# The last block of each attention unit as 64 by 64 corners, and the natural k of two units turned on chip

## The chip, the core and the metric

The kernel runs on one core of a Trainium2 chip. The core has five engines with queues of their own: TensorE (PE; its weight loads are listed apart, as PEld), VectorE (DVE), ScalarE (ACT), GpSimd (POOL) and SyncE (SP, which issues most transfers). The metric is device time in microseconds for one launch, over several executions; lower is better.

## What is computed

A linear attention with decay over 8 batches, 8 heads, 576 positions and 64 dimensions, whose output is the input of a mixture of eight experts with a fixed capacity of 576 tokens each:

```python
scores = scale * np.matmul(q, k.transpose(0, 1, 3, 2))
Dmat = np.where(rel >= 0, gamma[:, None, None] ** rel[None, :, :], 0.0)   # rel = query position - key position
x = np.matmul(scores * Dmat, v)                      # then (batch, position) rows of 512
# tokens are given to experts in order of their gate logits, 576 to each expert
h = np.maximum(x[mask] @ w1[e], 0.0); out[mask] = h @ w2[e]
```

All of it is in float32.

## The kernel before

The attention is cut into 16 **units** (u): a pair of batches times a pair of heads. A unit's sequence is 9 blocks of 128 columns for each head. Blocks 0 to 7 are 128 positions of one batch, b = 0 and 1 in turn. The last one, block 8, holds the last 64 positions of both batches side by side. q and k come in transposed (`qin`, `kin`: the dimensions of two heads on 128 partitions), v comes in natural form (`vin`), and k a second time in natural form (`nin`, 512 KB a unit), since the running state needs it.

A unit has two **halves**, g = 0 and 1. In half g of unit u TensorE runs, in program order:

- `from_states(u, g)`: what earlier blocks contribute through the running state, q times `st` into the PSUM tile `px` (L713). In half 1 there are 12 matmuls: 8 with 128 columns and 4 with 64 columns, the last four for block 8. Each takes 64 rows and 64 columns of the array, at four places in turn.
- `scores` of the next half (L678: 8 matmuls, 64 rows by 128 columns of the array, two at a time), and in half 0 also of block 8 (L683: 2 matmuls over all 128 by 128 pairs of block 8, into spare columns of `px`).
- `update(n, .)`: two adds of four matmuls to the running state in PSUM (L699); ACT then copies the scaled state to `st` (L702).
- `from_blocks(u, g)`: the masked scores times v into `px` (L722), and in half 1 block 8 too (L728: 4 matmuls over 128 rows and 64 columns).

DVE multiplies the scores by the decay mask (`masks`: L690 into `am` for four blocks, L688 into `at` for block 8, 256 columns). Half of what L683 computes pairs positions of different batches; the mask holds zeros there. ACT copies the finished `px` to `xT` (`keep`, L737). In some halves the gate's logits follow (`logits`, L754) and DVE prepares the routing (`fills`).

POOL scales q (`qscale`, L654) and the natural k (`kscale`, L659, into `ks`) of unit u+2 at the end of unit u. For units 0 and 1 no natural k is loaded: `kscale_pe` turns four blocks of `kin` by TensorE into the PSUM tile `pT` (L667), and DVE scales them into `ks` (L668).

Nothing but the text of the program sets the order: each engine runs its own instructions as they were written, SP's transfers among them, and semaphores hold one engine to another. A tile has a few buffers, and whoever writes a buffer anew waits for the last reader of the old content: `kin`, `qin` and `vin` have 4, `nin` has 3, `px` has 2, `sc` has 1. The loads of unit u+4 are written in unit u: k after the scores of half 0, q and natural k in half 1. v of unit u+3 comes at the start of unit u.

After the 16 units come the routing and the eight experts, each with two layers of matmuls (L1190, L1258).

Of the kernel before, what the change touches and what calls it, by code (L numbers as in the profile page):

```python
# [10 lines left out]
F32 = mybir.dt.float32  # L11
# [3 lines left out]
ALU = mybir.AluOpType  # L15
# [3 lines left out]
B, H, S, D = 8, 8, 576, 64  # L19
NP, HP, NB = 4, 4, 9  # L20
# [4 lines left out]
def consts_np():  # L25
    h = np.arange(H); g = (1.0 - 2.0 ** (-5.0 - h)).astype(np.float64)
    p = np.arange(128); gh = g.reshape(HP, 2)[:, p // 64].T
    i = np.arange(128)
    ex = 0.125 * gh[:, :, None] ** i
    ss = gh[:, :, None] ** (128.0 * np.arange(1, 5))  # L30
    c = np.arange(4)
    ks = g.reshape(HP, 1, 1, 2)[None] ** (-(128.0 * c[None, None, :, None, None] + p[:, None, None, None, None]))
    ks = np.broadcast_to(ks, (128, HP, 4, 2, 2))
    f = lambda a: np.ascontiguousarray(a, dtype=np.float32).reshape(128, -1)
    g1 = g[None] ** (-p[:, None].astype(np.float64)); g2 = g[None] ** (-(p[:, None] % 64).astype(np.float64))
    return np.concatenate([f(a) for a in (ks, ss, g1, g2, ex)], axis=1)

RUNS = ((0, 256, 0), (256, 512, 1), (512, 832, 0), (832, 1152, 1))
# [554 lines left out]
def attention(tc, nc, P, qk, vk, cst_d, wg_d, rf, xd, Lg, raw):  # L593
# [5 lines left out]
    m1, m2 = [cst[:, x:x+1024].rearrange("p (h j q) -> p h j q", h=4, j=2) for x in (NC, NC + 1024)]  # L599
    tri = raw()[:, :128].bitcast(BF16).rearrange("p (m q) -> p m q", m=2)  # L600
    for m in range(2):
        nc.vector.tensor_scalar(tri[:, m], P['it'], 0.0, None, op0=ALU.is_ge)
    nc.vector.memset(tri[:64, 1, 64:], 0.0)

    def decays(hp):
        for m, x in enumerate((80, 88)):
# [64 lines left out]
    def scores(u, g):  # L671

        t = SC[u, g] = P['pp'].tile([128, 2, 512], F32, name="sc", tag="sc")
        k, q = LD[u, 'k'], LD[u, 'q']
        for j in range(4):
            for h in range(2):
                r = slice(64*h, 64*h+64)
                nc.tensor.matmul(t[:, h, 128*j:128*j+128], blk(k, 4*g+j)[r], blk(q, 4*g+j)[r], start=(j == 0), stop=True, skip_group_check=True)  # L678
        if g:
            PX[u, 1] = P['pp'].tile([128, 2, 512], F32, name="px", tag="px", bufs=2)  # L680
            for h in range(2):
                r = slice(64*h, 64*h+64)
                nc.tensor.matmul(PX[u, 1][:, h, 384:], blk(k, 8)[r], blk(q, 8)[r], start=True, stop=True, skip_group_check=True)  # L683

    def masks(u, g):
        if g:
            AT[u] = P['w'].tile([128, 2, 128], F32, name="at", bufs=1)
            nc.vector.tensor_tensor(AT[u], PX[u, 1][:, :, 384:], m2[:, u % HP], op=ALU.mult)  # L688
        a = AM[u, g] = P['w'].tile([128, 2, 4, 128], F32, name="am", bufs=2)
        nc.vector.tensor_tensor(a, SC[u, g].rearrange("p h (j q) -> p h j q", q=128),  # L690
                                m1[:, u % HP, :, None, :].to_broadcast([128, 2, 4, 128]), op=ALU.mult)
# [11 lines left out]

    def from_states(u, g):

        if g == 0:
            PX[u, 0] = P['pp'].tile([128, 2, 512], F32, name="px", tag="px", bufs=2)
        q = LD[u, 'q']
        for c, o, n in ((1, 128, 128),) if g == 0 else ((2, 0, 128), (3, 128, 128), (4, 256, 64)):
            for b, h in ((0, 0), (1, 1), (1, 0), (0, 1)):  # L710
                r, y = slice(64*h, 64*h+64), 64*(h ^ b)
                x = 256*c + 128*b if c < 4 else 1024 + 64*b
                nc.tensor.matmul(PX[u, g][y:y+64, b, o:o+n], SS[u, c-1][r, b], q[r, x:x+n],  # L713
                                 start=(c == 1 + g), stop=False, skip_group_check=True)

    def from_blocks(u, g):
        v = LD[u, 'v']
        for j in range(4):
            c, b = divmod(j, 2)
            for h in range(2):  # L720
                y = 64*(h ^ b)
                nc.tensor.matmul(PX[u, g][y:y+64, b, 128*c:128*c+128], blk(v, 4*g+j)[:, 64*h:64*h+64], AM[u, g][:, h, j],  # L722
                                 start=False, stop=True, skip_group_check=True)
        if g:
            for b in range(2):
                for h in range(2):
                    y = 64*(h ^ b)
                    nc.tensor.matmul(PX[u, g][y:y+64, b, 256:320], blk(v, 8)[:, 64*h:64*h+64], AT[u][:, h, 64*b:64*b+64],  # L728
                                     start=False, stop=True, skip_group_check=True)

    def keep(u, g):
        bp, hp = divmod(u, HP)
# [133 lines left out]
    def ahead(u):  # L866
        if u == 0:
            load(2, "qknv")
            load(3, "qkn")
        if u + 3 < 16:  # L870
            load(u + 3, "v")
        if u == 1:
            R.fetch(nc, rf)
            for b in range(2):
                for h in range(2):
                    nc.sync.dma_start(wg[64*h:64*h+64, :, b, 0:8], wg_d.rearrange("(hp h p) e -> h p hp e", h=2, p=64)[h ^ b])
# [13 lines left out]
    qscale(1, (0, 512))  # L890
    qscale(1, (512, 1024), (1024, 1152))
    last = 15
    for u in range(16):
        ahead(u)
        for g in range(2):
            n, m = (u, u + 1)[g], (1, 0)[g]
            from_states(u, g)
            if u == g == 0:
                update(0, 1)
                kscale_pe(0, 1)  # L900
            if g and u + 4 < 16:
                load(u + 4, "qn")
            if u == 0 and g:
                kscale_pe(1, 1)
            if n <= last:
                scores(n, m)
                masks(n, m)
                update(n, 2 - 2*g)
            elif g:
                here[0] = P['pp'].tile([128, 2, 512], F32, name="px", tag="px", bufs=2)  # L910
                logits(NP-1, 0, 4)
            from_blocks(u, g)
            if u == g == 0:
                kscale_pe(1, 0)
            if not g and u + 4 < 16:
                load(u + 4, "k")
            if n <= last:
                update(n, 3 - 2*g)
            end = u == last and g
            here[0] = PX[u, g]  # L920
            if end:
                keep(u, g)
                R.kp = False
                logits2(NP-1, 0, 4)
                rest(R.count_first(27, 31))
                logits(NP-1, 4, 9, range(HP - 1))
                fills(u, g)
                break
            fills(u, g - 0.5)
            keep(u, g)  # L930
            fills(u, g)
            for f in later:
                f()
            later.clear()
            if g and u + 2 <= last:
                qscale(u + 2, (0, 512), (512, 1024), (1024, 1152))
                kscale(u + 2, 0, 8)
                kscale(u + 2, 8, 16)
    bp = NP-1
    left = [(y, b) for y, x in ((bp - 1, range(6, NB)), (bp, range(NB))) for b in x]  # L940

# [459 lines left out]
```

## Time and profile before

| | us |
|---|---|
| three runs, median (lowest to highest) | 598.72 (597.72 to 598.8) |
| the profiled execution, its own time | 598.47 |
| its span, first to last instruction | 596.3 |
| TensorE busy | 587.7 (99%) |
| VectorE busy | 410.5 (69%) |
| ScalarE busy | 256.4 (43%) |
| GpSimd busy | 242.9 (41%) |
| chain that ended last: share of TensorE | 93% |

The granted TensorE clock is full (9 tenths or more) in all 40 slices of the page. The page's DMA row reads 8 or 9 tenths in the first four slices, and 79.30 MB are read from HBM in all. A busy share tells little by itself here: which engine is waited for is read from the waits and from the chain of work.

### The profile page before, as it was taken

The numbers are of one execution on the slowest core, as the hardware profiler recorded it, in microseconds if no ns is written. First come the engines' busy times: TensorE is split into PE (matmuls) and PEld (weight loads), VectorE is DVE, ScalarE is ACT, GpSimd is POOL, SyncE is SP. The second block draws the span as 40 slices with busy tenths as digits, with TensorE's granted clock in tenths as the row PEclk, the third lists the DMA queues.
The fourth block names the chain that finished last, engine by engine and source line by source line (L and its number), as shares of the span: only waits on it lengthen the run. The fifth ranks groups of instructions, "written<-read, shape, count | busy, mean of one in ns | idle before, by whom it ended". The sixth has DMA issues, their size and how long they took to land.

```text
span 596.3 us, 15107 instructions
## 1 busy us (share of the span) xinstructions
PE 587.7 (99%) x5877; PEld 514.6 (86%) x5877; DVE 410.5 (69%) x1484; ACT 256.4 (43%) x464; POOL 242.9 (41%) x318
## 2 busy tenths in 40 slices
PE   8999999999999999999999999999999999999997
PEld 5888888885798899879988998898789889989976
DVE  5447687896999788878976876788588557543400
ACT  3534333334572664435561654266245334433310
POOL 3777666415311641451342153134214754841012
PEclk9999999999999999999999999999999999999999
DMA  8999999646865897795894699289928833430001
GB/s 329 411 377 406 309 402 370 206 129 229 270 157 111 263 272 158 254 243 146 217 295 143 155 243 255 83 195 245 253 79 192 261 110 102 154 135 27 1 27 53
DMA packets 48745, 123.27 MB, mean 207 GB/s; under 512 B 6946, under 2 KB 19746, under 8 KB 48674
## 3 DMA queue, kind: packets, MB, share of 16 engines
q1 hardware_dynamic: 35554, 79.05, 37.6%
q0 software_dynamic: 12976, 43.00, 31.2%
q8 instruction: 46, 0.75, 0.5%
q10 hardware_dynamic: 144, 0.26, 0.1%
q14 instruction: 25, 0.20, 0.1%
HBM read 79.30 MB, written 18.87 MB: 165 GB/s over the span
## 4 chain that ended last, share of the span: by engine, by line
PE 93%; issue 3%; DMA 2%; POOL 1%; DVE 1%; ACT 0%; POOLq 0%; SPq 0%; DVEq 0%; ACTq 0%
PE ph L1190 35%; PE py L1258 31%; PE sc L678 6%; PE px L722 5%; PE pS L699 3%; PE px L713 3%; PE r L403 2%; PE pt L1145 2%; PE pT L754 2%; PE pT L794 1%; POOL out_y L1215 1%; DMA xg<-xd,idx 1%; PE px L728 1%; DMA raw<-in_w 1%; PE px L683 1%
## 5 line engine op out<-in xcount | busy, mean ns | idle before, releaser
L1258 PE MATMUL py<-w2h,hb 128*128 128x512 f32 x560 | 180.8, 395 | 0.0
L1190 PE MATMUL ph<-xh,w1h 128*128 128x320 f32 (+1 forms) x512 | 152.2, 301 | 0.0
L1190 PE MATMUL ph<-xl,w1h 128*128 128x320 f32 (+1 forms) x512 | 149.2, 296 | 0.0
L1190 PE MATMUL ph<-xh,w1l 128*128 128x320 f32 (+1 forms) x512 | 149.1, 296 | 0.0
L1258 PE MATMUL py<-w2l,hb 128*128 128x512 f32 (+1 forms) x312 | 121.8, 390 | 0.0
L1258 PEld LDWEIGHTS py<-w2h,hb 128*128 128x128 f32 x560 | 102.8, 188 | 21.9
L1194 ACT ACTIVATE hb<-ph 128x256 fp32r<-128x256 f32 (+1 forms) x128 | 52.3, 408 | 106.7 <-PE ph L1190 104.3
L1190 PEld LDWEIGHTS ph<-xh,w1h 128*128 128x128 f32 x512 | 96.2, 190 | 1.1 <-ACT xh L1154 0.5
L1190 PEld LDWEIGHTS ph<-xl,w1h 128*128 128x128 f32 x512 | 96.2, 190 | 0.3
L1190 PEld LDWEIGHTS ph<-xh,w1l 128*128 128x128 f32 x512 | 96.1, 190 | 0.0
L1215 POOL DMA_INDIRECT out_y<-yt,idx x39 | 39.5, 1014 | 117.7 <-ACT yt L1275 58.0
L1199 DVE SCALAR_TENSOR_TENSOR hb<-ph,hb 128x256 fp32r<-128x256 f32 (+1 forms) x192 | 57.9, 350 | 23.8 <-ACT hb L1194 23.3
L1258 PEld LDWEIGHTS py<-w2l,hb 128*128 128x128 f32 (+1 forms) x312 | 55.2, 177 | 12.4
L1275 ACT ACTIVATE yt<-py 128x512 f32<-128x512 f32 x31 | 18.5, 598 | 93.5 <-PE py L1258 61.6
L654 POOL TENSOR_TENSOR qin<-qin,cst 128x512 f32<-128x512 f32 (+2 forms) x47 | 45.3, 991 | 32.2 <-DMA qin<-in_qk 32.2
L702 ACT ACTIVATE st<-pS,cst 128x128 f32<-128x128 f32 x64 | 23.5, 367 | 73.1 <-PE pS L699 73.1
L690 DVE TENSOR_TENSOR am<-sc,cst 128x1024 f32<-128x1024 f32 x32 | 39.0, 1219 | 21.4 <-PE sc L678 17.6
L1070 POOL DMA_DIRECT2D w2l<-raw x24 | 21.6, 902 | 71.7 <-ACT w2l L1069 39.0
L1091 POOL DMA_INDIRECT xg<-xd,quarter x36 | 37.2, 1033 | 18.4 <-ACT hb L1194 7.6
L1104 POOL DMA_INDIRECT xg<-xd,idx x25 | 25.4, 1015 | 41.6 <-DVE room L552 17.6
L678 PE MATMUL sc<-qin,kin 64*128 64x128 f32 x512 | 37.6, 285 | 0.1
L1060 ACT ACTIVATE w1h<-raw 128x1024 fp32r<-128x1024 f32 x32 | 33.6, 1055 | 5.5 <-DMA raw<-in_w 5.5
(235 smaller groups left out, 926.5 us busy)
## 6 DMA issues: line engine op xcount, KB each, us to landing
raw<-in_w SPq DMA_DIRECT2D x56, 512.0 KB, 5.9
w2l<-raw POOLq DMA_DIRECT2D x24, 512.0 KB, 5.3
w1l<-raw POOLq DMA_DIRECT2D x22, 512.0 KB, 6.8
qin<-in_qk SPq DMA_DIRECT2D x14, 576.0 KB, 8.7
kin<-in_qk SPq DMA_DIRECT2D x14, 576.0 KB, 8.7
vin<-in_vk SPq DMA_DIRECT2D x14, 576.0 KB, 8.7
nin<-in_vk SPq DMA_DIRECT2D x14, 512.0 KB, 8.4
xd<-raw SPq DMA_DIRECT2D x36, 128.0 KB, 5.5
```

Source lines behind the costliest of these rows:

```text
L654: by.tensor_tensor(x, x, e[:, None, :n].to_broadcast([128, (b-a)//n, n]), op=ALU.mult)
L678: nc.tensor.matmul(t[:, h, 128*j:128*j+128], blk(k, 4*g+j)[r], blk(q, 4*g+j)[r], start=(j == 0), stop=True, skip_group_check=True)
L690: nc.vector.tensor_tensor(a, SC[u, g].rearrange("p h (j q) -> p h j q", q=128), m1[:, u % HP, :, None, :].to_broadcast([128, 2, 4, 128]), ...
L722: nc.tensor.matmul(PX[u, g][y:y+64, b, 128*c:128*c+128], blk(v, 4*g+j)[:, 64*h:64*h+64], AM[u, g][:, h, j], start=False, stop=True, skip_g ...
L1060: A.activation(hi, raw, AF.Copy)
L1091: nc.gpsimd.indirect_dma_start(out=t[:, k, :], out_offset=None, in_=xq[:, :], in_offset=bass.IndirectOffsetOnAxis(ap=quarters[e][:, v:v+1] ...
L1104: nc.gpsimd.indirect_dma_start(out=xg[:n, j, :], out_offset=None, in_=xd[:, :], in_offset=bass.IndirectOffsetOnAxis(ap=found[e][:n, j:j+1] ...
L1190: T.matmul(ps, w, x, start=(k == 0), stop=(k == 11))
L1194: A.activation(hb[:, f, c], ps, AF.Relu)
L1199: V.scalar_tensor_tensor(hb[:, f, to+a:to+b], ps[:, a:b], 0.0, hb[:, f, 256*s+a:256*s+b].bitcast(F32), op0=ALU.max, op1=ALU.subtract)
L1215: st = nc.gpsimd.indirect_dma_start(out=to[:, :], out_offset=bass.IndirectOffsetOnAxis(ap=(at or found[e])[:n, t:t+1], axis=0), in_=y[:n], ...
L1258: T.matmul(ps[:m], a, w, start=(k == 0), stop=(k == last), skip_group_check=True)
```

## The change

It has two parts. **Corners:** block 8's scores are computed only for pairs of the same batch: per head and batch one matmul of 64 rows, 64 array columns and 64 moving columns (L711 in the new numbering), placed after `from_states` of half 1. The mask is 128 by 128 where it was 128 by 256 and is written right there. The products with v become `tail` (L730 in the new numbering): 64 rows, 64 array columns, 64 moving columns, after the second `update` of half 1. **Turned k:** the natural k of units 3 and 4 is no longer loaded nor scaled by POOL; `kscale_pe` makes it, in unit u's half 1 for blocks 0 to 3 of unit u+2, and in the next unit's half 0 for blocks 4 to 7. Since block 8 of k is now read in half 1, the load of k for unit u+4 moves from half 0 to half 1, ahead of q.

```diff
+    g2[64:] = g2[64:].reshape(64, HP, 2)[:, :, ::-1].reshape(64, H)
...
-    nc.vector.memset(tri[:64, 1, 64:], 0.0)
+    nc.vector.tensor_copy(tri[64:, 1, :64], tri[64:, 1, 64:])
...
-        if g:
-            PX[u, 1] = P['pp'].tile([128, 2, 512], F32, name="px", tag="px", bufs=2)
-            for h in range(2):
-                r = slice(64*h, 64*h+64)
-                nc.tensor.matmul(PX[u, 1][:, h, 384:], blk(k, 8)[r], blk(q, 8)[r], start=True, stop=True, skip_group_check=True)
...
-        if g:
-            AT[u] = P['w'].tile([128, 2, 128], F32, name="at", bufs=1)
-            nc.vector.tensor_tensor(AT[u], PX[u, 1][:, :, 384:], m2[:, u % HP], op=ALU.mult)
...
+        if g:
+            k = LD[u, 'k']
+            for h, b in ((0, 0), (1, 1), (0, 1), (1, 0)):
+                r, y = slice(64*h, 64*h+64), 64*b
+                nc.tensor.matmul(PX[u, 1][y:y+64, h ^ b, 384:448], blk(k, 8)[r, y:y+64], blk(q, 8)[r, y:y+64],
+                                 start=False, stop=True, skip_group_check=True)
+            AT[u] = P['w'].tile([128, 2, 64], F32, name="at", bufs=1)
+            nc.vector.tensor_tensor(AT[u], PX[u, 1][:, :, 384:448], m2[:, u % HP, :, :64], op=ALU.mult)
...
-        if g:
-            for b in range(2):
-                for h in range(2):
-                    y = 64*(h ^ b)
-                    nc.tensor.matmul(PX[u, g][y:y+64, b, 256:320], blk(v, 8)[:, 64*h:64*h+64], AT[u][:, h, 64*b:64*b+64],
-                                     start=False, stop=True, skip_group_check=True)
+    def tail(u):
+        v = LD[u, 'v']
+        for b, h in ((0, 0), (1, 1), (1, 0), (0, 1)):
+            r, y = slice(64*b, 64*b+64), 64*(h ^ b)
+            nc.tensor.matmul(PX[u, 1][y:y+64, b, 256:320], blk(v, 8)[r, 64*h:64*h+64], AT[u][r, h ^ b],
+                             start=False, stop=True, skip_group_check=True)
...
-            load(3, "qkn")
+            load(3, "qk")
...
+    turned = (3, 4, )
...
-                load(u + 4, "qn")
+                load(u + 4, "kq" if u + 4 in turned else "kqn")
...
-            if not g and u + 4 < 16:
-                load(u + 4, "k")
+            if u + 1 + g in turned:
+                kscale_pe(u + 1 + g, 1 - g)
...
+            if g:
+                tail(u)
...
-                kscale(u + 2, 0, 8)
-                kscale(u + 2, 8, 16)
+                if u + 2 not in turned:
+                    kscale(u + 2, 0, 8)
+                    kscale(u + 2, 8, 16)
```

TensorE in an undisturbed unit, before: half 1 of a unit and then half 0 of the next. A row is a line of the kernel, the operation, its output and inputs, the shape of the output and the count.

```order
L713 MATMUL px<-qin,st 64x128 x8
L713 MATMUL px<-qin,st 64x64 x4
L678 MATMUL sc<-qin,kin 128x128 x8
L699 MATMUL pS<-vin,ks 64x64 x4
L722 MATMUL px<-am,vin 64x128 x8
L728 MATMUL px<-at,vin 64x64 x4
L699 MATMUL pS<-vin,ks 64x64 x4
L713 MATMUL px<-qin,st 64x128 x4
L678 MATMUL sc<-qin,kin 128x128 x8
L683 MATMUL px<-qin,kin 128x128 x2
L699 MATMUL pS<-vin,ks 64x64 x4
L722 MATMUL px<-am,vin 64x128 x8
```

The same stretch of the changed kernel, with the transposes that stand in both halves here (half 1 of unit 2, where unit 4's first blocks are turned, and half 0 of unit 3):

```order
L705 MATMUL px<-qin,st 64x64 x4
L711 MATMUL px<-qin,kin 64x64 x4
L679 MATMUL sc<-qin,kin 128x128 x8
L692 MATMUL pS<-vin,ks 64x64 x4
L722 MATMUL px<-am,vin 64x128 x8
L668 MATMUL pT<-ident,kin 128x128 x4
L692 MATMUL pS<-vin,ks 64x64 x4
L730 MATMUL px<-at,vin 64x64 x4
L705 MATMUL px<-qin,st 64x128 x4
L679 MATMUL sc<-qin,kin 128x128 x8
L692 MATMUL pS<-vin,ks 64x64 x4
L722 MATMUL px<-am,vin 64x128 x8
```

The scores of block 8 moved from behind the scores of half 0 to the end of `from_states` of half 1; the products with v moved behind the second `update`, next to the following `from_states`; the transposes stand between `from_blocks` and the second `update`, in four halves in all. Elsewhere the rows are the same.

SP in the first unit, before (from the load of q for unit 3 on):

```order
L622 DMA qin<-in_qk 128x1152
L622 DMA kin<-in_qk 128x1152
L622 DMA nin<-in_vk 128x1024
L622 DMA vin<-in_vk 128x1152
L622 DMA kin<-in_qk 128x1152
L622 DMA qin<-in_qk 128x1152
L622 DMA nin<-in_vk 128x1024
L622 DMA vin<-in_vk 128x1152
```

and in the changed kernel:

```order
L623 DMA qin<-in_qk 128x1152
L623 DMA kin<-in_qk 128x1152
L623 DMA vin<-in_vk 128x1152
L623 DMA kin<-in_qk 128x1152
L623 DMA qin<-in_qk 128x1152
L623 DMA vin<-in_vk 128x1152
```

Two loads of 512 KB are gone, both behind the k of unit 3 (the second row of each), and nothing ahead of it moved.

## Rows read from the trace of the kernel before

**Rows 1.** Busy time of each engine by stretch: length, busy (instructions), clock, DMA, GB/s

```profile
core 0: us, PE busy (x) PEld busy (x) DVE busy (x) ACT busy (x) POOL busy (x), PEclk, DMA share, GB/s
12.71:123.75 111.04, 110.94 (x2318) 98.36 (x2321) 75.12 (x170) 44.53 (x111) 70.97 (x72) 1.00 0.96 348
57.16:64.03 6.87, 6.87 (x144) 6.08 (x148) 5.80 (x14) 3.22 (x8) 4.92 (x5) 1.00 1.05 390
```

**Rows 2.** Waits from 12.5 to 124 us: engine, line, releaser, total us, times, longest

```profile
POOL qin L654 <- DMA qin<-in_qk: 24.5, 14, 5.9
...
PEld px L713 <- ACT st L702: 1.6, 9, 0.2
```

**Rows 3.** Chain of work, 56 to 73.2 us: start, us, what, records (two a matmul)

```profile
57.16 0.87 PE px L713 x24
58.03 1.09 PE sc L678 x16
59.12 0.38 PE pS L699 x8
59.50 0.88 PE px L722 x16
60.38 0.23 PE px L728 x8
60.61 0.23 PE pS L699 x8
60.84 0.38 PE px L713 x8
61.22 1.09 PE sc L678 x16
62.31 0.22 PE px L683 x4
62.54 0.38 PE pS L699 x8
...
64.03 0.87 PE px L713 x24
...
72.22 0.71 PE px L713 x24
```

**Rows 4.** Chain of work, 10 to 13 us, around the transposes of unit 1

```profile
10.86 0.88 PE px L722 x16
11.74 0.59 PE pT L667 x4
12.32 0.38 PE pS L699 x8
```

**Rows 5.** Chain of work at the end of the attention

```profile
126.66 0.23 PE px L728 x8
126.89 1.34 PE pT L754 x32
```

**Rows 6.** Chain of work, 22 to 25 us, half 1 of unit 1

```profile
22.13 0.38 PE pS L699 x8
...
23.38 0.23 PE px L728 x8
```

**Rows 7.** The load of unit 3's k: its issue on SP, and its time to landing

```profile
11.75 0.33 SPq L622 DMA_DIRECT2D kin<-in_qk  x1
...
kin<-in_qk SPq DMA_DIRECT2D x1, 576.0 KB, 10.9
```

**Rows 8.** POOL's scaling of unit 2's natural k, from the order of time

```profile
18.84 2.05 POOL L659 TENSOR_TENSOR ks<-nin,cst 128x512 f32<-128x512 f32 x2
```

**Rows 9.** DVE: one mask with its wait at 118.89 us; two groups, 5 to 20 us

```profile
118.89 1.22 DVE L690 TENSOR_TENSOR am<-sc,cst 128x1024 f32<-128x1024 f32 x1 [0.50 <-PE sc L678]
...
L668 DVE TENSOR_TENSOR ks<-pT,cst 128x512 f32<-128x512 f32 x4 | 2.8, 691 | 2.9 <-PE pT L667 2.9
L688 DVE TENSOR_TENSOR at<-px,cst 128x256 f32<-128x256 f32 x2 | 0.8, 425 | 2.9 <-PE px L683 2.9
```

More of the change, by code (lines that the diff above doesn't have):

```diff
@@ L704, in from_states @@
     def from_states(u, g):
-        if g == 0:
-            PX[u, 0] = P['pp'].tile([128, 2, 512], F32, name="px", tag="px", bufs=2)
+        PX[u, g] = P['pp'].tile([128, 2, 512], F32, name="px", tag="px", bufs=2)
         q = LD[u, 'q']
```

## The prediction

> **What bounds the kernel now.** I read the busy times by stretch first, because the change touches only the attention. From half 1 of unit 0 to half 1 of unit 15 (fifteen units) TensorE is busy 110.94 of 111.04 us [rows 1]. A busy share alone proves little, so the waits came next: over the same time no row of the waits names TensorE's matmuls, and the only wait of its weight loads that sums to over a microsecond beside issue time is for ACT's copy of the state, 9 times, 1.6 us in all [rows 2]. POOL, in contrast, waits 24.5 us for q [rows 2], and the transfer engines are busy all the time (share 0.96 and 1.05) [rows 1]. So the loads run late for POOL, but not for TensorE. The chain of work confirms it: a unit is 6.87 us from one `from_states` to the same one a unit later, and its pieces, all of TensorE, follow without a gap: 0.87 + 1.09 + 0.38 + 0.88 + 0.23 + 0.23 + 0.38 + 1.09 + 0.22 + 0.38 + 0.88 + 0.23 (the last two like those above them) = 6.86 [rows 3]. The attention is bound by how many matmul records TensorE streams and by how often it changes the shape of its tiles. Transfers, POOL and DVE are cover.
>
> One piece holds a wait. The 24 records of `from_states` in half 1 take 0.87 us where they follow `update` at once and 0.71 where logits stand ahead of them [rows 3]: the last eight wait for ACT's copy of the state that `update` has just added to. The change writes nothing between that `update` and these records, so the 0.16 us stays in every unit that has it now.
>
> **The change part by part.** *Corners.* Taken away in each unit: L683, 4 records, 0.22 us, and L728, 8 records, 0.23 us [rows 3]. Both stand in TensorE's stream with no gap around them, so both come off the path. Added: twice 8 records of 64 columns on 64 by 64 tiles, four tiles at a time. That form is in the trace, as the last eight records of `from_states`. Its price: 8 records of 128 columns take 0.38 us with the change of tile shape; 16 of 128 and 8 of 64 take 0.71 without the wait [rows 3]. The further 8 and 8 thus take 0.33, and by their columns (two to one) 0.22 and 0.11. Both new groups stand directly beside a `from_states`, in its tile shape: the scores behind it, the `tail` ahead of it. So neither adds a change of shape, and a unit saves 0.22 + 0.23 - 0.11 - 0.11 = 0.23 us. In unit 15 no `from_states` follows the `tail`; logits do. There the `tail` pays a change of shape, which is 0.15 us (`update` takes 0.38 us behind a group of another shape, 0.23 behind one of its own [rows 3]): 0.26 in place of 0.23 [rows 5], and unit 15 saves 0.08. Sum: 15 x 0.23 + 0.08 = 3.5 us.
>
> *Turned k.* Four calls of four transposes. The trace has the same call in the same place, between `from_blocks` and `update`, for unit 1: 0.59 us for the transposes, and the `update` behind them takes 0.38 [rows 4] instead of 0.23. Each call adds 0.59 + 0.15 = 0.74 us, four 2.96. The least I can make of it is 0.59 each (2.36), if the change of shape were to cost nothing; there is no row by which it would cost more. Nothing hides it, since TensorE has no idle time there [rows 1].
>
> What this buys lies off the path: two loads of 512 KB fewer (1.05 MB, 2.7 us of transfer at the 390 GB/s of the unit measured [rows 1]) and four POOL instructions fewer (2.05 us a unit [rows 8]). The tightest use of POOL's work that I found is unit 2's natural k: it is ready at 18.84 + 2.05 = 20.89, and the `update` of unit 2 begins at 22.13 [rows 6, 8], 1.2 us later; but that load is ahead of the ones taken out and gains nothing. Work that came in time before is not worth more for coming earlier, so I cost this at nothing.
>
> *Moves.* The mask of block 8 (DVE) goes from half 0 to half 1, ahead of the mask of the next scores, and shrinks from 256 to 128 columns. The 256 take 0.425 us [rows 9]; 0.3 is an estimate from that and from 1.22 for 1024. In half 1 DVE sits idle before the next mask, 0.50 us in one of the fullest halves [rows 9], so it fits. Behind it on DVE is that mask, and for that the next scores but one; in half 0 the mask now starts earlier by what went. `from_blocks` now also waits for the small mask, since it writes the same `px`, but some 1.5 us later (scores 1.09 and `update` 0.38 [rows 3]). If DVE's idle time were gone, each 0.1 us of lateness beyond that would be TensorE's. DVE's four products of the turned k (0.691 us each [rows 9]) fall in units 1 to 3, before the routing's work is there. On SP the load of k moves behind half 0's writes of finished rows and ahead of q, whose landing moves by that one load at most, about 1.5 us (576 KB at 390 GB/s). Only POOL waits for it, with microseconds to spare.
>
> *A new wait.* The first turned blocks need unit 3's k in half 1 of unit 1. It was issued at 11.75 and landed 10.9 us later [rows 7], at 22.65. TensorE got to that place, the start of L728, at 23.38 [rows 6]; by then it will have saved two L683 and one L728 and run three new groups: 0.44 + 0.23 - 0.33 = 0.34 us, so it gets there at 23.04. It holds by 0.4 us. Nothing that the change takes out stands ahead of this load, so it lands no earlier. Behind the waiting transposes stands everything on TensorE.
>
> The sum: -3.5 + 2.96 = -0.6 us. On the profiled execution (598.47, of which 596.3 is span) that is 597.9; on the median of the runs, 0.25 above the profiled one, **598.1**. The later phases follow the attention's end by chains of their own, and I let them shift as a block.
>
> **The rivals.** *The corners don't run four abreast (slower).* In the corner scores, the tiles of head 0 and of head 1 write different partitions of one PSUM bank at the same time. If they had to take turns, 8 records would cost what L728's do two at a time, 0.23 us [rows 3], for both groups 2 x 0.12 x 16 = 3.8 us more: **601.9**. The point from which the change loses is near: 0.13 us a group in place of 0.11 uses up the 0.6. For it: this order of the four places is not in the trace. Against it: `from_states` has the same two row tiles in one bank and still shows 24 records in 0.71 us. [...] Chance 0.06.
>
> *Unit 3's k comes late.* A load that lands one load later than here (1.5 us) would hold TensorE 1.1 us: up to **599.2**, within 0.2% of before. For it: the margin of 0.4 us and a saturated transfer stage; against it: what stands ahead of the load is the same. Chance 0.10.
>
> *The loads were the bound after all (faster).* If late loads held TensorE in a way that the waits don't show, the 2.7 us of transfer would come off: **595.4**. For it: the DMA share and POOL's waits. Against it: no wait of TensorE in fifteen units, and a unit that is the sum of its own pieces. Chance 0.06.
>
> **How the numbers follow.** The forecast has 0.78. The runs before spread by some 0.5 us to either side, and about what a measurement of this kernel can tell from no change is 0.2%, 1.2 us. A gain of 0.6 with that spread, and with sixteen rounded pieces, passes 1.2 in part: I put 0.12 of the 0.78 there. Faster: 0.12 + 0.06 = 0.18. Within 0.2%: 0.66 + 0.10 = 0.76. Slower: 0.06. The range takes the forecast with the transposes at their least (597.5) and the spread of the runs below it, 596.9, and up to the late k with some of that spread, 599.4; it leaves out the first and the third rival.
>
> **What would show it.** In the profile after: an undisturbed unit of 6.64 us; L711 and L730 with 8 records in 0.11 us each in the chain; four groups of transposes of 0.59 us, each with an `update` of 0.38 behind it; the `from_states` of half 1 still 0.16 us longer without logits ahead; the attention's last `px` group ending at 126.3 where it ended at 126.89 [rows 5]; no wait of TensorE for DMA near 23 us. It would be wrong if the new groups took 0.2 us or more each, if TensorE waited for `kin` or for the small mask, or if the attention ended 0.6 us earlier and the rest took it back.

## The result, and the profile after

The changed kernel takes 602.15 us (median of 11 runs, 601.16 to 607.47) where the kernel before takes 598.80 on the same chip (11 runs, 597.72 to 601.36): a ratio of 1.0062, 95% interval 1.0042 to 1.0081. It is slower by 0.6%; the prediction said 598.1 and gave this side a chance of 0.06. The profiled execution took 601.71, of which 599.9 is span.

The busy time by stretch comes first, as in [rows 1]: the changed kernel from half 1 of unit 0 to half 1 of unit 15, the same fifteen units.

```profile
core 0: us, PE busy (x) PEld busy (x) DVE busy (x) ACT busy (x) POOL busy (x), PEclk, DMA share, GB/s
12.34:126.06 113.72, 110.98 (x2394) 96.52 (x2397) 77.97 (x174) 44.65 (x111) 67.30 (x68) 1.00 0.94 333
```

Before, these units took 111.04 us and TensorE was busy 110.94 of them. Now they take 113.72, and it is busy 110.98. So TensorE's work has not grown; by this view it stands still for 2.74 us where it stood for 0.10. The page's busy times of the whole program say the same: 587.7 us in both, in a span 3.6 us longer. But busy time shows too little of a standstill: in this trace the matmul records of the attention last 0.22 to 0.30 us each on the mean and overlap (`scores`: 0.285 us each, and sixteen in 1.16), so most of a short one counts as busy.

The chain of work shows that the new pieces cost what was forecast. A stretch of it in the changed kernel (start, us, what, records):

```profile
34.15 0.88 PE px L722 x16
35.03 0.59 PE pT L668 x4
35.61 0.38 PE pS L692 x8
35.99 0.60 PE px L705 x16
36.59 0.02 issue
36.61 0.34 PE px L705 x8
36.96 0.12 PE px L711 x8
37.08 1.09 PE sc L679 x16
38.17 0.38 PE pS L692 x8
38.55 0.88 PE px L722 x16
39.42 0.23 PE pS L692 x8
39.66 0.28 PE px L730 x8
39.93 0.22 PE px L705 x8
```

Transposes 0.59 with an `update` of 0.38 behind them, corner scores (L711) 0.12, `tail` and the first state products 0.28 + 0.22 = 0.50 (forecast 0.11 + 0.38). One piece is longer: `from_states` of half 1 takes 0.96 us here (35.99 to 36.96), where 0.87 was forecast to stay.

What is new shows in the waits of TensorE's matmuls from 12 to 128 us (engine, line, what released it: us in all, times, longest), of which [rows 2] had none:

```profile
PE pS L692 <- POOL ks L660: 1.5, 2, 1.0
PE sc L679 <- DMA xd<-raw: 0.8, 1, 0.8
PE pT L756 <- issue: 0.2, 1, 0.2
```

Two names and a third row without one, and the names don't bear a second look. The longest wait, in order of time (start, us, engine, line, what; idle time before it and its releaser):

```profile
72.71 2.04 POOL L660 TENSOR_TENSOR ks<-nin,cst 128x512 f32<-128x512 f32 x2
...
82.59 1.16 PE L679 MATMUL sc<-qin,kin 64*128 64x128 f32 x16
82.73 0.29 DVE L714 TENSOR_TENSOR at<-px,cst 128x128 f32<-128x128 f32 x1 [1.12 <-PE px L711]
83.41 2.05 POOL L660 TENSOR_TENSOR ks<-nin,cst 128x512 f32<-128x512 f32 x2
83.68 0.13 PEld L692 LDWEIGHTS pS<-vin,ks 128*64 128x64 f32 x1
83.80 1.23 DVE L683 TENSOR_TENSOR am<-sc,cst 128x1024 f32<-128x1024 f32 x1 [0.78 <-PE sc L679]
84.76 0.39 PE L692 MATMUL pS<-vin,ks 128*64 128x64 f32 x7 [1.00 <-POOL ks L660]
```

The `update` at 84.76 belongs to unit 10. Its scaled k is the pair of POOL instructions at 72.71, done ten microseconds earlier; the pair at 83.41, which the view names, is unit 11's. The first weights of this very `update`, which are that scaled k, were already loaded at 83.68, and then nothing came for a microsecond. So it waited neither for POOL nor for data.

I then counted TensorE's records (MATMUL, LDWEIGHTS and its sequencer's own) from the start of the program, and gave each standstill of over 0.3 us its place in a block of 256:

```
changed kernel         before
us      line  place    us      line  place
54.39   L722   192     54.73   L678   192
60.92   L692   194
73.06   L756   193
84.76   L692   192
91.20   L679   195
108.56  L730   192
```

Four places out of 256, six times out of six, at five different lines. (Where a block begins in this count is read from the standstills themselves; nothing else in the trace shows it.) The list of DMA queues has a queue for something of that size (packets, MB, share of the 16 engines over the program):

```profile
q8 instruction: 47, 0.77, 0.5%
```

Its 47 packets have 16384 bytes each, and there is one for every 256 records of TensorE (12034 records here; before, 46 packets for 11874), about one every 6 us in the attention. There each starts after TensorE has passed such a boundary, 0.2 to 5.1 us after it in the two kernels, and each of the six standstills ends 1.15 to 1.54 us after the packet has landed that started behind the boundary before. So I read such a packet as the block of instructions that TensorE needs from the next boundary on. In the changed kernel, from 82.3 to 83.4 us (queue: packets, MB, share of the 16 engines):

```profile
q1 hardware_dynamic: 101, 0.42, 99.1%
q8 instruction: 1, 0.02, 5.5%
```

and from 78.17, where the block before was entered, to 82.35:

```profile
q1 hardware_dynamic: 408, 1.61, 101.0%
```

The queue of the loads holds the engines, and the block that TensorE needs at 84.76 starts to move only at 82.36, 4.2 us after the boundary. It has landed at 83.32, and TensorE goes on 1.44 us later.

My theory after this, called A in the expectations: with the transfers full, a block takes about 6 us from its boundary to its use, an estimate from these traces (wait 3 to 4.2, transfer 0.95, 1.2 to 1.5 until TensorE goes on). The kernel before used up a block in 6 us, just at the limit: of the first 17 blocks that were fetched from 11 us on, ten landed only 1.3 to 1.6 us ahead of their use. The corners put eight more records into a unit that has 0.23 us less work, so TensorE reaches the end of a block before the next one is there. The rival B: data come late at these places, since the loads were moved.

### The profile page after: what moved, and what is told of

It reads as the page before. It is cut to its first block, busy times and chain, and to the rows that moved or that the text cites. A ratio compares the mean times of both kernels' runs of the same rounds, so it can differ in the third digit from the quotient of the medians.

```text
span 599.9 us, 15277 instructions
## 1 busy us (share of the span) xinstructions
PE 587.7 (98%) x5957; PEld 512.2 (85%) x5957; DVE 413.4 (69%) x1488; ACT 256.5 (43%) x464; POOL 238.8 (40%) x314
## 4 chain that ended last, share of the span: by engine, by line
PE 84%; DMA 6%; issue 4%; DVE 2%; POOL 2%; SPq 1%; ACT 1%; POOLq 0%; DVEq 0%; ACTq 0%
PE ph L1196 33%; PE py L1264 30%; PE sc L679 5%; PE px L722 4%; PE pS L692 3%; PE px L705 2%; DMA xd<-raw 2%; PE r L404 2%; DMA qin<-in_qk 2%; DMA w2l<-raw 1%; PE pt L1151 1%; PE pT L756 1%; PE pT L668 1%; POOL out_y L1221 1%; DMA raw<-in_w 1%
```

## The experiments

A table first, of all runs but the three `throttle` ones. Each row is one profiled execution, and not all on the same chip. "Attention" runs from the first state product to the last `px` record. "At boundaries" is what the intervals between matmul records exceed the median of the same interval in the same kernel, summed over the places 188 to 202 of the blocks, from 12 to 128 us; it is good to some tenths. "Left" is the attention less that. "Fetch" is the mean time from place 192 to the start of the next 16384-byte packet, 36 to 108 us, good to 0.2. "Behind" is the profiled time less the attention's end. The `light` kernels compute other values and so another routing; only their attention is compared. (The 125.02 and 127.44 us in the first expectations are one record near that end, in before and in the changed kernel; the durations of the table take their place.)

```
kernel            attention  at boundaries  left   fetch  profiled  behind
before              119.14      1.34       117.80  3.27   598.47    471.6
changed kernel      121.76      3.91       117.85  3.07   601.71    472.4
after_again         123.87      5.15       118.72  3.17   605.73    474.0
corners_only        119.69      4.74       114.95  2.98   601.62    473.5
turned_only         121.02      0.00       121.02  1.93   600.41    470.9
tail_only           118.76      2.63       116.13  3.46   597.49    470.9
before_dense        124.69      0.30       124.39  2.71   604.79    471.5
after_shift         119.89      2.35       117.54  2.89   602.34    471.0
after_light         118.96      0.42       118.54  1.78
before_light        118.45      0.21       118.24  2.13
corners_light       118.15      3.53       114.62  2.52
corners_lighter     116.31      1.12       115.19  1.74
after_halves        119.76      1.68       118.08  2.69   599.28    471.3
before_halves       118.63      0.00       118.63  2.21   597.95    471.4
after_split         123.21      3.69       119.52  2.89   605.28    472.8
corners_split       118.27      3.63       114.64  3.09   599.15    473.3
before_split        120.86      2.98       117.88  3.37   599.66    471.4
```

"Left" is no clean measure of the work, since it varies by 2 us among kernels with the same instructions: the first state products of unit 0 and what follows up to its half 1 took `after_again` 0.8 us longer, behind a late load of q, and `after_split` 1.95 us longer, with matmuls at about half the rate (16 records of `scores` in 2.01 us, at a granted clock that reads 1.00; the cause is open). A better one is the shortest time that each unit takes, from its `from_states` of half 1 to the next unit's, in any of the runs with the same TensorE instructions, summed over the attention: 118.07 us for the kernel before (four runs), 117.88 for the changed one (six), 114.85 for the corners alone (four), and 121.02 for `turned_only` (one run, without standstills). By it the kernel before loses 1.1 us to standstills and the changed one 3.9.

**The two halves of the change.** `corners_only` loads natural k again; `turned_only` is the kernel before with the turned units.

```
corners_only:  -    turned = (3, 4, )            turned_only, on before:
               +    turned = ()                  +    turned = (3, 4, )
               -    load(3, "qk")                -    load(3, "qkn")
               +    load(3, "qkn")               +    load(3, "qk")   and the k loads and kscale_pe of the change
```

> The 64x64 corners alone; the natural k of units 3 and 4 is loaded as before. By the work terms of the prediction alone the attention's last px group ends 3.5 us earlier than before (121.5 where before has 125.02) and the kernel takes about 595.3 us. Theory A (TensorE runs out of instructions: they come in blocks of 256, and a block takes about 6.2 us to come while the transfers are full): the same stalls as in the changed kernel, every one 192 to 195 records into a block of 256 of TensorE's stream, over 3 us in all, and the kernel within 1 us of before or slower. Theory B (data late because loads were moved and left out): the stalls change with the loads; those by unit 3 and 4 go, and most of the gain of 3.5 us shows.

> The kernel before with the natural k of units 3 and 4 turned by TensorE, and its k loads moved as in the change; block 8 as before. By the work terms: +2.96 us, 601.8 us, the attention's last px group at 128.0. Theory A: the four transposes groups are slow per instruction, so the stream is no denser than before: at most 0.5 us of stalls, 601.3 to 602.3. Theory B: the moved k loads make data late, stalls of over 2 us as in the changed kernel and over 603.5 us.

Measured: `corners_only` 599.97 us against 599.05, ratio 1.0020 (0.9997 to 1.0042), with the natural k loaded again and nothing turned. Its standstills of over 0.3 us are all at places 192 and 193, in other blocks and at other points of the program than those of the changed kernel. Now the waits view calls them "issue", which is time in which the engine waited for nothing that the profile shows. The longest in the chain of work:

```profile
60.42 0.44 PE px L722 x6
60.86 1.20 issue
62.07 0.71 PE px L722 x9
```

It lies in the middle of a group of sixteen records of one line, whose mask and v had served the six records ahead of it. No load and no other engine can be late there. `turned_only` took 600.27, ratio 1.0016 (0.9998 to 1.0034), not 601.8: its transposes cost what was forecast (0.59 and 0.38 in its chain), and up to unit 4 it is 2.93 us behind the kernel before. Later it gets back more than one, since no block comes late in it any more. So the kernel before loses 1.1 to 1.3 us to late instructions of its own. Theory B expected over 603.5; it falls here, since the loads are moved and nothing stands still.

**The stream alone.** `tail_only` gives the kernel before the shorter `tail`, with the same number of records; `before_dense` gives it more records.

```
tail_only:     r = slice(64*b, 64*b+64) if u < 15 else slice(0, 128)
               nc.tensor.matmul(PX[u, 1][y:y+64, b, 256:320], blk(v, 8)[r, ...], AT[u][r, h, 64*b:64*b+64], ...)   # behind update
before_dense:  for i in range(4):
                   nc.tensor.matmul(PX[u, 1][:64, 0, 448:456], q[:64, :64], q[:64, 0:8], ...)
```

> The kernel before, with only the four products of block 8 by v (L728) cut to 64 rows and put behind update, where they run four abreast (0.11 us in place of 0.23); the scores of block 8 stay whole, so TensorE has not one instruction more than before. By the work terms: 15 x 0.12 = 1.8 us off the attention, 597.2 us. Theory A (TensorE runs out of instructions): the same 292 records in less time is a denser stream, so stalls 192 to 195 records into a block take back 0.8 us or more; the attention (first state product to last px record) takes 118.3 to 119.1 us where before takes 119.14, and the kernel 598.2 to 599.2. Rival (only added instructions cost): 117.3 us and 597.2.

> The kernel before with four more small products a unit (64x64 by 8 columns, into columns of px that nobody reads), 16 more records a unit, loads untouched. By work alone: about 0.11 us a unit, 1.8 us in all, the attention 119.14 + 1.8 = 120.9 us. Theory A: a fuller stream, more than that: 2 to 4 us of stalls 192 to 195 records into a block of 256, the attention 122 to 124 us. Theory B (moved or late loads): no stalls, since no load is moved; 120.9.

`tail_only` took 598.20 against 598.91, ratio 0.9997 (0.9981 to 1.0012). The work fell by 1.7 us, as costed, and the boundaries took 1.3 of it back: no instruction more, no load moved, and still no gain to be measured. `before_dense` missed. My estimate for its products was far off: they cost 6.6 us (0.41 a unit) and not 1.8; why was not tested. So the stream did not get fuller: 300 records in an undisturbed unit of 7.27 us are the rate of 284 in 6.87. The standstills went (0.30), with 0.4 us a unit more for the same loads. It tells nothing on B, but it shows that more records do not by themselves bring standstills.

**The place.** `after_shift` puts half a block of records ahead of unit 0's masks; `after_again` is the changed kernel once more.

```
     scores(0, 0)
+    for i in range(32):
+        nc.tensor.matmul(PT[:64, 0:64], LD[0, 'k'][:64, :64], LD[0, 'k'][:64, 64:128], start=True, stop=True, ...)
     masks(0, 0)
```

> The changed kernel with 32 small products (64x64 by 64 columns, into a bank that is written anew behind them) between unit 0's first scores and its masks: 128 records more ahead of everything else, half a block. Their own time is under 4 us and lies ahead of unit 0. Theory A: the stalls stay 192 to 195 records into a block of TensorE's stream and so come at other lines of the program, half a block (some 3 us) earlier in it; none stays at the first update behind scores of unit 10 (L692) by virtue of the place. Theory B (data late at these places): they stay at the same lines of the same units, and move to other positions in the blocks.

> The changed kernel once more, for how much of its stalls is chance: if the stalls depend on when a fetch meets a full queue, they come again 192 to 195 records into blocks, but not all in the same blocks, and the attention takes 120 to 123 us (121.76).

With the program half a block further on, every standstill of over 0.3 us between 12 and 128 us lies at 192 to 195 again and at other lines (L705 at 55.79, 95.63 and 107.32). The wait for POOL at unit 10 is gone without anything having been done to POOL. `after_again`, in 123.87 us where up to 123 was expected, has standstills at the same lines in five of the six blocks, and two more; the view names POOL's `ks` at unit 10 again:

```profile
86.20 1.05 POOL L660 TENSOR_TENSOR ks<-nin,cst 128x512 f32<-128x512 f32 x1
...
86.37 0.34 PE L692 MATMUL pS<-vin,ks 128*64 128x64 f32 x5 [1.09 <-POOL ks L660]
```

The POOL instruction that it names runs from 86.20 to 87.25, past the record that it is said to release. So the program fixes where they can come, and the moment which of them come and how long they are: 3.91 us in one execution, 5.15 in the other.

**The transfers.** Four kernels leave loads out. The `light` ones scale unit 2's natural k in place of later ones; `corners_lighter` uses old v as well.

```
+        if u >= 3:
+            what = what.replace("n", "")         # corners_lighter: also "v", from unit 4 on
-    LD[u, 'n']
+    LD[min(u, 2), 'n']
```

> The changed kernel without the loads of natural k from unit 5 on (POOL scales unit 2's k instead, so the values are others, and with them the routing behind the attention). TensorE's instructions are the same. Theory A: the transfers are no longer full, a block of instructions comes sooner, the stalls at 192 to 195 go, and the attention's last px group ends at 125.02 - 0.6 = 124.4 or earlier (127.44 in the changed kernel). Theory C (the stalls are a matter of TensorE's own records, such as the corners' bank): they stay, 127.4.

> The kernel before without the loads of natural k from unit 3 on (POOL scales unit 2's k instead; other values and routing). Theory A: before has only one stall of this kind (0.17 us at 54.7), so the attention's end moves by 0.2 us at most (124.8 to 125.1). If loads bound TensorE in a way that the waits hide: over 1 us earlier.

> The corners alone, without the loads of natural k from unit 3 on (POOL scales unit 2's k instead, so the values are others, and with them the routing behind the attention). TensorE's instructions are those of corners_only. The attention's work without stalls is 118.07 - 3.5 = 114.6 us. Theory A: with 0.52 MB a unit fewer in the transfers the blocks come sooner, at most 1 us of stalls is left, 114.6 to 115.6 us in the attention, where corners_only has 119.69 and before_light 118.45. If the corners' saving were not there: about 118.

> The corners alone, without the loads of natural k from unit 3 on and without those of v from unit 4 on (older tiles are used in their place, so the values and the routing are others). TensorE's instructions are those of corners_only. Taking only natural k out left 3.5 us of stalls (corners_light, 118.15 us), against what theory A was given to expect there. With 1.1 MB a unit fewer the transfers have spare time between loads. Theory A: fetches start within 2 us of a boundary on the mean, stalls of under 1 us, the attention takes 114.6 to 115.6 us. If it stays at 118 with the transfers half empty, then full transfers are not what delays the blocks.

Busy times from 36 to 110 us, one line from each kernel's view by stretch, in the order before, changed kernel, corners_only, turned_only, corners_light, corners_lighter:

```profile
36.00:110.00 74.00, 73.90 (x1570) 65.73 (x1567) 54.02 (x117) 28.33 (x69) 52.67 (x54) 1.00 1.00 372
```

```profile
36.00:110.00 74.00, 71.30 (x1586) 62.70 (x1586) 52.95 (x129) 28.07 (x68) 49.24 (x50) 1.00 0.99 357
```

```profile
36.00:110.00 74.00, 71.06 (x1562) 62.59 (x1563) 52.63 (x114) 27.62 (x67) 52.83 (x53) 1.00 1.01 373
```

```profile
36.00:110.00 74.00, 74.00 (x1570) 65.44 (x1566) 55.30 (x129) 28.18 (x69) 47.02 (x48) 1.00 0.99 349
```

```profile
36.00:110.00 74.00, 72.26 (x1616) 63.22 (x1616) 53.57 (x116) 28.06 (x69) 52.02 (x54) 1.00 0.90 298
```

```profile
36.00:110.00 74.00, 73.53 (x1658) 64.83 (x1654) 55.45 (x118) 28.48 (x70) 52.55 (x53) 1.00 0.74 220
```

The first number behind the length is TensorE's busy time, the last two are the transfer engines' share and GB/s. In `after_light` the standstills at boundaries fall from 3.91 to 0.42 us and the attention by 2.8. It is 0.2 us shorter than before's and not the 0.6 asked for: 0.6 us went in and behind a wait that is put down to POOL, at another place (231 of a block), and the work itself is only 0.2 us less. `before_light` gains 0.7 us, more than the 0.2 that I gave it, by the 1.1 us at boundaries that I had not yet counted. `corners_light` is a plain miss: with a share of 0.90 it keeps 3.53 us of standstills. One fetch there still waited 5.07 us and cost 1.3. Only `corners_lighter`, with a share of 0.74, gets them down to 1.12, both while a fetch waited 3.9 to 4.0 us. Then the attention takes 116.31 us, 2.8 less than before's, and an undisturbed unit in its chain is the predicted 6.64 us. So the corners' saving is real, and no run with full transfers got it in the kernel's time. The mean share is a poor measure of it; how much was queued when a boundary was crossed was not measured.

**What a fetch waits behind.** The `halves` cut each load into two; the `split` ones keep the loads and lay the columns out in two halves in DRAM, so that packets are half as large; the `throttle` ones let two or three loads be outstanding.

```
halves:    for a, b in ((0, n//2), (n//2, n)): nc.sync.dma_start(t[:, a:b], src[:, a:b])
split:     src, t2 = src.rearrange("(a p c) -> p a c", a=2, p=128), t.rearrange("p (a c) -> p a c", a=2)
throttle:  if len(hist) >= 3: nc.sync.dma_start(gate[:, len(hist):len(hist)+1], hist[-3][0:1, 0:1])
```

> The changed kernel with each load of q, k, v and natural k cut into two of half the columns: the same bytes in packets of half the size, on the same queue. If the block of instructions waits behind a number of data packets, it comes 1 to 2 us sooner, the stalls shrink by over half, and the attention takes 118 to 119.5 us (121.76 in the changed kernel), the kernel 598 to 600. If it waits behind bytes, nothing changes: 121.8 and 602. If smaller packets cost transfer time, the stalls grow: over 122.5.

> The kernel before with the loads cut in the same way. turned_only showed the attention's work to be 121.02 - 2.94 = 118.1 us, so before loses about 1.1 us to late instructions. If half the packet means a shorter wait: 118.1 to 118.5 us in the attention and 598.0; else 119.1 and 599.0; over 119.5 if smaller packets cost transfer time.

> The changed kernel with q, k, v and natural k laid out in DRAM in two halves of the columns: the same number of loads, of bytes and of loads outstanding, but packets of 2304 and 2048 bytes in place of 4608 and 4096. If a block of instructions waits behind a number of packets: the mean wait from the boundary to the fetch falls from 3.07 us to under 2.3, the attention takes 118.5 to 120 us (121.76 in the changed kernel), the kernel 599 to 600.5. If it waits behind bytes: 3.1 us, 121.8 and 602. If smaller packets cost so much transfer that data is late: waits by semaphores, over 122.5.

> The corners alone, natural k of units 3 and 4 loaded, with the packets halved in the same way. By a number of packets: the wait falls from 2.98 us to under 2.3, half or more of the 5.1 us of stalls goes, 115.5 to 117.5 us in the attention (119.69 in corners_only), the kernel 596 to 598, less than before's. By bytes: 119.7 and 600.

> The kernel before with the packets halved in the same way. It loses 1.1 us to late instructions, so by a number of packets 118.1 to 118.5 us in the attention (119.14) and 598.0; by bytes 119.1 and 599.0. What it gains or loses is also the price of the smaller packets alone.

> The corners alone, and SP holds each whole load back until the one three before it has landed (a 4-byte copy out of that load's tile stands ahead of it on SP's queue). Theory A with the addition that a block of instructions waits behind the loads that are outstanding: with at most three outstanding, the time from a block's boundary to the next fetch falls from 2.98 us (mean of corners_only between 36 and 108 us) to under 2, most of the 5.1 us of stalls goes, the attention takes 114.6 to 116.5 us (119.69 in corners_only), the kernel 595 to 597, less than both. If the outstanding loads don't matter: 119.7 and 600. If three loads can't keep the transfers full: data late, waits of TensorE for kin, vin or POOL's ks, over 121.

> The same with two loads outstanding. Theory A with the addition: fetches start within 1.5 us of a boundary, no stalls 192 to 195 records into a block, but the transfers lose throughput (two loads are 2.9 us of transfer at 390 GB/s); if that is enough for the attention, 114.6 us and 595; if not, TensorE waits for data by semaphores, at other positions in the stream, and the attention takes over 118.

> The kernel before with the same hold of three loads. It loses about 1.1 us to late instructions (119.14 against 118.07 of work), so no more than that comes back: 118.1 to 118.5 us and 598.0. If the gain of the throttled corners came from something else than the stalls, such as better timed data, before would gain as much as they do, over 2 us.

Half the packet changes nothing in the wait: 2.89, 3.09 and 3.37 us with `split`, 3.07, 2.98 and 3.27 without. So it isn't a number of packets. `corners_split` (600.75, ratio 1.0037, 1.0006 to 1.0068), `after_split` (603.79, 1.0063, 1.0039 to 1.0086) and `before_split` (600.46, 1.0003, 0.9979 to 1.0028) gain nothing. The `halves` do lower the wait, to 2.69 and 2.21. They also halve what can be outstanding: in the traces of before and of the changed kernel SP's transfers go on eight semaphores in turn, and up to 130 us no issue came ahead of a landing that the trace shows of the transfer eight back (in the changed kernel v is issued at 8.23, the eighth before it lands at 8.21). Bytes outstanding would explain both; I did not measure them apart. Against the kernel before, `after_halves` took 601.19 (ratio 1.0049, 1.0033 to 1.0065), no clear gain on the changed kernel's 1.0062, and `before_halves` 602.07 (1.0058, 1.0041 to 1.0075), a loss. Their profiled executions were the fastest of each; where the slower ones lose was not seen.

The `throttle` kernels show what a wait for data looks like. They took 625.01, 656.92 and 624.05 us. The time to the next fetch did fall, to 1.6, 1.2 and 1.8 us on the mean, and no block came late in the two with corners (up to 122 us they landed at least 2.3 us ahead of their use, where standstills have 1.2 to 1.5). Now data came late. The waits of TensorE's matmuls in `corners_throttle3`, 12 to 150 us:

```profile
PE sc L683 <- POOL qin L659: 12.4, 6, 5.5
PE pS L696 <- POOL ks L664: 10.9, 9, 1.5
PE pS L696 <- DMA vin<-in_vk: 0.5, 1, 0.5
```

They name what fits late loads, recur at the same two lines, and lie at any place of a block (149, 182, 167, 29, 129, ...). With three loads outstanding the transfers moved 275 GB/s in place of 373:

```profile
36.00:110.00 74.00, 57.39 (x1183) 50.52 (x1185) 42.02 (x97) 21.26 (x52) 39.32 (x40) 0.91 0.87 275
```
So the transfers at 373 GB/s brought TensorE's data in time and its blocks late (`corners_only`, 4.74 us at boundaries), and at 275 GB/s the blocks in time and the data late; I tried two and three loads outstanding and none between those and the eight of the kernels, and no version that keeps all loads beats the kernel before by more than can be measured.

## Why the prediction was wrong

*What bounds the kernel.* This is the step that failed. I took "no wait by a semaphore, and pieces that follow without a gap" for proof that TensorE's work sets the time and that transfers are cover. The rows were right, and there was a second bound just beneath the first: blocks of instructions that came every 6 us to an engine that used one up every 6 us. The row that showed the transfers at a share of 0.96 to 1.05 [rows 1] was read for its loads alone. The kernel before even had one standstill at 54.73, in the middle of a group of `scores`, which I read over:

```profile
53.88 0.75 PE sc L678 x9
54.73 0.60 PE sc L678 x6
```

The group takes 1.45 us from 53.88 to its end, where 1.09 is usual, and such standstills took 1.1 to 1.3 us in all, most of which the busy time hid.

*Corners.* Forecast 3.5 us; measured as work 3.2 (118.07 less 114.85). Most of the 0.3 lies in units 0 and 1, which save 0.13 each and not 0.23: there `from_states` of half 1 waits 0.09 us longer. In the full stream 3.4 us comes back as added standstills, and the attention of `corners_only` took 0.55 us more than before's, one execution of each; over all runs it is 0.2% slower, with an interval that reaches below no change. "Both come off the path" was the sentence that had to be costed a second time, against the supply of instructions.

*Turned k.* Forecast 2.96; measured as work 2.95 (121.02 less 118.07), and 1.9 net, since no block came late. "I cost this at nothing" was wrong by 1.1 us in the kernel that has no corners. Its fetches wait 1.93 us on the mean and not 3.27; why those of later units do too, whose loads are all there, was not tested. In the changed kernel the two together take the work from 118.07 to 117.88: -0.2 where -0.6 was forecast. The standstills make the rest and more: 3.9 less 1.1 are 2.8 us, and 2.8 less 0.2 are the attention's 2.6.

*Moves and the new wait.* Right but for one size. No wait for `kin` near 23 us (`from_blocks` ends and the transposes begin at 23.09), the small mask takes 0.29 us, and the `from_states` of half 1 still waits for ACT, in some early units by 0.25 us and not 0.16.

*The end.* The last `px` group ends at 129.36, where 126.3 was forecast. The attention starts 0.15 us earlier than before's, so it is 2.62 us longer. The rest of the time shifted as a block within what it varies by: from the attention's end to the end of the execution 470.9 to 474.0 us in all rows above, 471.6 before and 472.4 after. The 0.8 between them can't be told from that spread.

*The rivals.* Corners that take turns: no, L711 takes 0.12 us. Late k of unit 3: no. "The loads were the bound after all" had the right resource and the wrong sign: loads held TensorE in a way that the waits did not show, but through its instructions, and the change made it worse.

## What to carry to other kernels

When an engine has no idle time and the transfers are full, ask what its instructions need: count its records per microsecond, and see in the list of DMA queues how long after a boundary the instruction packets start. In these runs a stream that is shorter, but no poorer in records, gained nothing measurable (`tail_only`, ratio 0.9997), and fewer bytes in the transfers gave the time back (`corners_lighter`, 116.31 us of attention against 119.69 in `corners_only`); fewer records were not tried. If a wait's named releaser was done long before, or falls in the middle of a group, put the place of each standstill in the stream beside the others: here the same place modulo a block meant instructions and not data, and data that were truly late showed at any place.

## What the chip did that I had not expected

In these traces a block of 256 TensorE records goes with one 16384-byte packet, which waits some 3 us on the mean (3.27 before, 3.07 in the changed kernel) and up to 5.1 while loads fill the transfers, and 0.2 us where none is left (125.78 us in the changed kernel: the packet starts 0.18 later, though small stores keep the engines' share at 0.89). It takes 0.9 to 1.7 us in the two kernels' attention, and TensorE went on no earlier than 1.15 us after it had landed. With packets of the loads half as large the wait was 2.89, 3.09 and 3.37 us, where it was 3.07, 2.98 and 3.27. And the clock fell where data were truly late: in `corners_throttle3`, from 36 to 110 us, with TensorE busy 57.39 of 74 us, the granted clock is 0.91 on the mean, and in `corners_throttle2`, with 57.44 busy, 0.84. It is 1.00 in the other six rows shown of that stretch.
